# Value chunks with their own keys first, a 128-partition load for the strided values, and a regrouped start

## The chip, the cores and the metric

The kernel runs on one core of a Trainium2 chip. The metric is device time in microseconds. Three runs of the kernel before took 277.28, 278.16 and 282.28 us; their median is 278.16 us.

## The reference

Sparse attention over 8 batches of 8 heads, 576 positions and 64 dimensions a head, followed by a feed-forward block with a product of two branches:

```python
batch, n_heads, seq, head_dim = (8, 8, 576, 64)
scores = scale * np.matmul(q, k.transpose(0, 1, 3, 2))
rel = pos[:, None] - pos[None, :]
mask_local = (rel >= 0) & (rel < 32)
mask_strided = (rel >= 0) & (pos[None, :] % 32 == pos[:, None] % 32)
# heads 0 to 3 take mask_local, heads 4 to 7 mask_strided
attn = softmax(np.where(mask, scores, -1e9))
x = (attn @ v).transpose(0, 2, 1, 3).reshape(B * S, H * D)    # 4608 tokens of 512
a = x @ w1                                                    # 512 by 1024
b = x @ w2
out = (a * b @ w3) @ w_out                                    # 1024 by 1024, 1024 by 512
```

All inputs and the output are float32.

## The kernel before

Work is done for pairs of heads. A batch has four: `hp` 0 and 1 are local, 2 and 3 are strided. `pairs[4 * b + hp]` holds them, and `p0` to `p8` are the first nine.

**Local heads** are cut into 6 chunks of 96 queries (`LQ`, `LT`). Chunk c is multiplied with the 128 keys that start 32 before it, so a local tile of values, `v16L`, holds in its first 32 partitions the last keys of the chunk before, and in partitions 32 to 127 its own 96. `load_vL` loads these 96 with one DMA a head into a float32 staging tile, casts them to float16 on GpSimd in two instructions, and copies the 32 shared rows on from the chunk before (on VectorE in batch 0, on GpSimd later).

**Strided heads** are cut into 8 chunks of 72 (`SQ`, `ST`) that hold every eighth position, so that row p of `v16S` holds positions 8p to 8p+7. `load_vS` loads two heads at a time, rows 0 to 63 and rows 64 to 71 in a DMA each, and casts them in one instruction.

For a pair, `ah_T`, `ah_R` and `ph_T` transpose q and k on TensorE (with `load_rest` for the positions from 512 on), `ah_scores` and `ph_S` form scores, ScalarE takes the exponential, and `ah_PV` or `ph_PV` multiplies with the values, which carry a column of ones for the sum. `norm` divides (VectorE), and `ph_T2` transposes the result into `xT`, the feed-forward's input. In batch 0 the mask is added as a bias on TensorE before the scores (`ah_S0`: `biasL`, `biasS`); from batch 1 on the exponentials are multiplied with `maskL` or `maskS` on VectorE (`ah_S`, `ph_soft`).

**The feed-forward** goes over 9 tiles of 512 tokens. `ab_parts` gives the units of a tile: for each of 8 columns of 128, two of the a product and two of the b product; ScalarE copies a out and VectorE multiplies. `w3` and `w_out` are folded into one matrix, `w34` (`fold_tr`, `fold_mm`), and `o_parts` gives the output product.

**Order.** TensorE runs in the order of the program (`pe` keeps it). The list `stream` holds batch 0's work by hand, with small idle matmuls (`warm`) in it, and the first six units of the feed-forward's first tile; the rest of that tile, the folding and the first output tile follow, with batch 1's work put between them by `plan` (unit number, function, pair). From batch 2 on, attention is spread over the feed-forward units by `host`. The other engines' orders are set by the framework's scheduler from the dependencies. All loads go through the SP queue in the order in which the program names them: q and k of batch 0, the rest, local values, the second heads' q and k, strided values, then the weights in blocks of 512 KB, then batch 1's inputs between the last blocks of w3. Staging tiles (`stgp`) are 9.

Of the kernel before, what the change touches and what calls it, by code (L numbers as in the profile page):

```python
# [19 lines left out]
def kernel(  # L20
# [33 lines left out]
    LC = 384  # L54
    PTG = S + 64
# [16 lines left out]

    def copy(eng, out, in_):
        if eng == "a":
            nc.scalar.copy(out=out, in_=in_)  # L75
        elif eng == "v":
            nc.vector.tensor_copy(out=out, in_=in_)  # L77
        else:
            nc.gpsimd.tensor_copy(out=out, in_=in_)  # L79
# [6 lines left out]
    maskL = consts.tile([P, LQ], FP16)  # L86
    nc.gpsimd.memset(maskL, 1.0)
    nc.gpsimd.affine_select(out=maskL, in_=maskL, compare_op=ALU.is_ge,
                            fill=0.0, base=32, pattern=[[1, LQ]], channel_multiplier=-1)
    nc.gpsimd.affine_select(out=maskL, in_=maskL, compare_op=ALU.is_ge,  # L90
                            fill=0.0, base=-1, pattern=[[-1, LQ]], channel_multiplier=1)

    sel = consts.tile([4, 18, 4], FP16)
# [5 lines left out]
    causal = consts.tile([SQ, SQ], FP16)  # L99
# [8 lines left out]
    biasL = consts.tile([P, LQ], FP16)  # L108
# [12 lines left out]
    nc.vector.memset(kT[:, 0:2, 0:32], 0.0)  # L121
    nc.vector.memset(kT[:, 2:4, S:KW], 0.0)
    for i in range(2):
        nc.vector.memset(v16L[i][:, :, :, D], 1.0)
        nc.vector.memset(v16L[i][0:32, :, 0, :], 0.0)
        nc.vector.memset(v16S[i][:, :, :, D], 1.0)
    for i in range(2):
        nc.vector.memset(ptms[i][:, S:PTG], 0.0)
        nc.vector.memset(ptms[i][:, 2 * S:PTW], 0.0)
# [55 lines left out]
    def load_vL(b, hps=(0, 1)):  # L185
        vt = v16L[b % 2]
        for hp in hps:
            hs = slice(2 * hp, 2 * hp + 2)
            st = stgp.tile([P, 2, LT, D], FP32, tag="stg")
            for h in range(2):  # L190
                nc.sync.dma_start(st[32:P, h], v[b, 2 * hp + h].rearrange("(t p) d -> p t d", p=LQ))
            for pr in (bass.ds(32, 32), bass.ds(64, 64)):
                nc.gpsimd.tensor_copy(out=vt[pr, hs, :, 0:D], in_=st[pr])  # L193
            copy("p" if b else "v", vt[0:32, hs, 1:LT, 0:D], vt[96:P, hs, 0:LT - 1, 0:D])

    def load_vS(b):
        vt = v16S[b % 2]
        for hp in range(2):
# [12 lines left out]
    for b in range(B):  # L211
        for hp in range(4):
# [3 lines left out]
            s.n1 = NB // s.w  # L216
            s.kr = P if s.local else SQ
            pairs.append(s)

    def half_rows(u):  # L220
        return slice(64 * u, 64 * u + 64)

    def ph_T(s, rest, pt):
# [20 lines left out]
        def out():  # L244
            for i, (eng, t) in enumerate(engs):
                pi = ps[:, :, i * 256:i * 256 + 256]
                if s.local:
                    c0 = 32 * i
                    copy(eng, t[:, s.hp, c0:c0 + NM].rearrange("x (u p c) -> x u p c", u=2, c=4),
# [6 lines left out]
            if rest:  # L256
                for i, (eng, t) in enumerate((("a", qT), ("v", kT))):
                    pr = ps[:, i, 512:768].rearrange("x (g r) -> x g r", g=4)
                    c0 = 32 * i + NM
                    copy(eng, t[:, 0:2, c0:c0 + NR], pr[:, 0:2])  # L260
# [5 lines left out]
    def ph_S(s):  # L266
        w, kr, n, n1 = s.w, s.kr, s.n, s.n1
# [4 lines left out]
        def sc(h, c):  # L272
            r = half_rows(h)
            o = sps[:, h, c * w:(c + 1) * w] if c < n1 else pt[:, h, LC:LC + w]
            pe(nc.tensor.matmul(o, kT[r, s.hp, w * c:w * c + P], qT[r, s.hp, w * c:w * c + w],  # L275
# [10 lines left out]

    def ph_soft(s, pt):
        w, kr, n, n1 = s.w, s.kr, s.n, s.n1
# [3 lines left out]
        mk = maskL if s.local else maskS  # L292
        m1 = 2 * n1 * w
        for lo, hi, src in ((0, m1, sps[0:kr, 0:2, 0:n1 * w]), (m1, 2 * S, pt[0:kr, :, LC:LC + w])):
            nc.scalar.activation(out=pte[0:kr, lo:hi], in_=src, func=AF.Exp, bias=0.0, scale=scale)  # L295
        nc.vector.tensor_mul(ptm[0:kr, 0:2 * S].rearrange("p (a x) -> p a x", x=w),  # L296
                             pte[0:kr].rearrange("p (a x) -> p a x", x=w),
                             _ap(mk, 0, [[mk.ap[0][0], kr], [0, 2 * n], [1, w]]))

    def ph_PV(s):  # L300
        w, kr, n, n1 = s.w, s.kr, s.n, s.n1
# [3 lines left out]
        for cs in (list(range(m)), list(range(m, n))):  # L305
# [8 lines left out]
            for i, c in enumerate(cs):  # L314
                for h in range(2):
                    c0 = (h * n1 + c) * w if c < n1 else (2 * n1 + h) * w
                    pe(nc.tensor.matmul(xps[:, h, i * 65:i * 65 + 65], s.ptm[0:kr, c0:c0 + P],  # L317
                                        vt[0:kr, 2 * (s.hp % 2) + h, c, :], start=True, stop=True))
            norm(s, xps[0:w, :, 0:l * 65], cs[0], l)

    def ah_T(s):
# [5 lines left out]
        for i, nm in enumerate("qk"):  # L327
            src = x16[(s.b, nm, s.hp // 2)]
# [4 lines left out]
        for i, t in enumerate((qT, kT)):  # L333
            eng = "v" if i and s.b == 0 else "a"
            if s.local:
                c0 = 32 * i
                copy(eng, t[:, s.hp, c0:c0 + NM].rearrange("x (p c) -> x p c", c=4),
# [5 lines left out]
    def ah_R(b):  # L343
# [11 lines left out]
        for i, t in enumerate((qT, kT)):  # L355
            c0 = 32 * i + NM
            eng = "v" if i and b == 0 else "a"
            parts = [(t[:, 0:2, c0:c0 + NR], pvs[0][:, :, i]),
# [7 lines left out]

    def ah_scores(s, g, outs, kn, first):
        w, m = s.w, s.n // 2
        for i in range(m):
            ks = w * (g * m + i)  # L370
            for h in range(2):
                r = half_rows(h)
                pe(nc.tensor.matmul(outs[h][0:kn, i * w:(i + 1) * w], kT[r, s.hp, ks:ks + kn],
                                    qT[r, s.hp, ks:ks + w], start=first, stop=first or i == m - 1))

    def ah_S0(s, g, wide=True):
        w, kr, m = s.w, s.kr, s.n // 2
        bias = biasL if s.local else biasS
        if wide:
            sps = psB.tile([P, 2, NB], FP32, tag="big", name="sps")  # L380
            outs = [sps[:, 0], sps[:, 1]]
        else:
            outs = [psF.tile([P, NB], FP32, tag="f", name="sph") for _ in range(2)]
# [378 lines left out]
```

## Time and profile before

| | |
|---|---|
| median of three runs | 278.16 us |
| profiled execution, its own time | 278.08 us |
| its span, first to last instruction | 276.2 us |
| granted TensorE clock over the span | 1.000 |
| TensorE busy | 261.8 us, 95% |
| ScalarE, VectorE busy | 147.8 and 147.6 us |
| GpSimd busy | 115.6 us, 42%, ending about 160 us in |
| DMA | 48.68 MB, mean 176 GB/s |

Times in lists are microseconds from the start of the span. L416 is line 416 of the kernel before. In the timeline a line has start, duration, engine, line, operation, output and input tile, their shapes, and in brackets the idle time of the engine before it with what ended it. In busy time by stretches, the columns are the stretch, its length, the busy time of PE (matmul), PEld (weight load), DVE (VectorE), ACT (ScalarE) and POOL (GpSimd), then the granted clock, the DMA share and the DMA rate in GB/s.

### The profile page before, as it was taken

The page shows a single profiled execution, that of the slowest core. Times are in us where ns is not written, and L with a number is a line of the kernel's source. Part 1 is how long each engine was busy: PE and PEld are TensorE (multiplying, and loading weights), DVE is VectorE, ACT ScalarE, POOL GpSimd, SP SyncE. Part 2 cuts the span into 40 slices and gives each one's busy share as a digit, 9 for nine tenths or more (in the row PEclk, how much of TensorE's full clock was granted, in tenths as well). Part 3 has the DMA queues.
Part 4 walks back from the last instruction along what each step waited for, and adds up shares of the span by engine and source line. Part 5 has one row for each costly group of instructions (what it writes and reads, how often), then busy time and mean ns, then how long its engine had stood idle before and what let it go on. Part 6 is the DMA issues. An engine that isn't in the chain of part 4 may idle for free.

```text
span 276.2 us, 6648 instructions
## 1 busy us (share of the span) xinstructions
PE 261.8 (95%) x2656; PEld 138.4 (50%) x2656; DVE 147.6 (53%) x281; ACT 147.8 (54%) x298; POOL 115.6 (42%) x134
## 2 busy tenths in 40 slices
PE   1888999999899999999999999999999999999995
PEld 0465455554455555555555455555555555444442
DVE  2465452566767556755874667466547653431430
ACT  1664335857666565555556655656665654324322
POOL 4586785787958762785693734100000000000000
PEclk9999999999999999999999999999999999999999
DMA  7999999999899859897997860310031012003004
GB/s 202 268 324 391 390 385 263 268 243 234 265 282 277 219 187 267 180 297 208 256 261 219 245 137 2 116 39 2 2 115 40 0 40 114 0 2 152 0 4 152
DMA packets 56753, 48.68 MB, mean 176 GB/s; under 512 B 29201, under 2 KB 45841, under 8 KB 56721
## 3 DMA queue, kind: packets, MB, share of 16 engines
q1 hardware_dynamic: 51536, 38.87, 53.3%
q10 hardware_dynamic: 5184, 9.37, 9.3%
q8 instruction: 21, 0.34, 0.6%
q14 instruction: 12, 0.09, 0.1%
HBM read 38.80 MB, written 9.44 MB: 175 GB/s over the span
## 4 chain that ended last, share of the span: by engine, by line
PE 88%; DVE 5%; ACT 3%; DMA 2%; issue 1%; SPq 1%; DVEq 0%
PE ops L490 24%; PE aps L463 23%; PE bps L474 22%; PE sps L317 4%; PE ps L434 3%; DMA st<-in_k_dram 2%; DVE xqs L427 2%; PE sps L275 2%; DVE ptm L403 2%; PE pt L232 2%; PE xps L416 1%; PE pt L275 1%; PE tps L331 1%; PE trp L532 1%; ACT pte L402 1%
## 5 line engine op out<-in xcount | busy, mean ns | idle before, releaser
L474 PE MATMUL bps<-xT,w2h 128*128 128x512 f16 x288 | 76.2, 379 | 0.0
L463 PE MATMUL aps<-xT,w1h 128*128 128x512 f16 x288 | 74.9, 380 | 0.7 <-ACT xT L441 0.7
L477 DVE TENSOR_TENSOR abt<-bps,asb 128x512 f16<-128x512 f32 x72 | 49.5, 687 | 41.8 <-PE bps L474 28.1
L467 ACT COPY asb<-aps 128x512 f32<-128x512 f32 x72 | 43.1, 598 | 46.7 <-PE aps L463 46.7
L490 PE MATMUL ops<-w,abt 128*128 128x512 f16 x280 | 67.1, 379 | 0.0
L79 POOL CAST t<-st 128x1024 f16<-128x1024 f32 (+1 forms) x46 | 45.6, 1000 | 25.1 <-DMA st<-in_q_dram 9.8
L463 PEld LDWEIGHTS <-w1h 128*128 128x128 f16 x288 | 26.5, 98 | 29.7
L474 PEld LDWEIGHTS <-w2h 128*128 128x128 f16 x288 | 26.2, 98 | 27.7 <-issue 1.2
L490 PEld LDWEIGHTS <-abt 128*128 128x128 f16 x280 | 25.3, 98 | 26.1
L193 POOL CAST v16L<-st 32x768 f16<-32x768 f32 (+1 forms) x32 | 27.4, 858 | 14.5 <-DMA st<-in_v_dram 8.4
L501 ACT COPY osb<-ops 128x512 f32<-128x512 f32 x35 | 20.6, 588 | 18.2 <-PE ops L490 18.2
L295 ACT ACTIVATE pte<-sps 128x960 f16<-128x960 f32 (+1 forms) x24 | 23.9, 995 | 11.6 <-PE sps L275 11.6
L427 DVE TENSOR_TENSOR xqs<-sps,rcp 96x768 f16<-96x768 f32 (+1 forms) x24 | 24.4, 1017 | 0.5
L204 POOL CAST v16S<-st 72x1024 f16<-72x1024 f32 x16 | 17.1, 1070 | 16.1 <-DMA st<-in_v_dram 8.0
L296 DVE TENSOR_TENSOR ptm<-pte,maskL 128x1152 f16<-128x1152 f16 x12 | 11.7, 975 | 21.4 <-ACT pte L295 21.4
L296 DVE TENSOR_TENSOR ptm<-pte,maskS 72x1152 f16<-72x1152 f16 x12 | 11.7, 973 | 20.2 <-ACT pte L295 20.2
L441 ACT COPY xT<-ps 128x576 f16<-128x576 f16 x16 | 10.3, 641 | 22.7 <-PE ps L434 22.7
L75 ACT COPY qT<-pt 128x256 f16<-128x256 f16 (+2 forms) x48 | 17.6, 409 | 3.3 <-DVE kT L77 2.9
L317 PEld LDWEIGHTS <-ptm 72*128 72x128 f16 (+1 forms) x336 | 13.1, 97 | 6.5 <-DVE ptm L296 2.0
L490 PE MATMUL ops<-woh,w3T 128*128 128x512 f16 x64 | 15.7, 380 | 0.2 <-DVE w3T L534 0.2
L434 PEld LDWEIGHTS <-xqs 72*128 72x128 f16 (+1 forms) x224 | 12.1, 97 | 7.5 <-DVE xqs L427 0.6
L434 PE MATMUL ps<-id,xqs 72*128 72x72 f16 (+1 forms) x224 | 13.5, 200 | 0.3 <-DVE xqs L427 0.3
(93 smaller groups left out, 252.4 us busy)
## 6 DMA issues: line engine op xcount, KB each, us to landing
out_dram<-osb ACTq DMA_DIRECT2D x35, 256.0 KB, 2.0
st<-in_q_dram SPq DMA_DIRECT2D x16, 512.0 KB, 5.2
st<-in_k_dram SPq DMA_DIRECT2D x16, 512.0 KB, 5.6
st<-in_moe_w_dram SPq DMA_DIRECT2D x16, 512.0 KB, 10.4
st<-in_v_dram SPq DMA_DIRECT2D x32, 144.0 KB, 5.7
st<-in_v_dram SPq DMA_DIRECT2D x16, 256.0 KB, 8.7
st<-in_moe_w_out_dram SPq DMA_DIRECT2D x4, 512.0 KB
st<-in_q_dram SPq DMA_DIRECT2D x8, 128.0 KB, 6.3
```

Source lines behind the costliest of these rows:

```text
L79: nc.gpsimd.tensor_copy(out=out, in_=in_)
L193: nc.gpsimd.tensor_copy(out=vt[pr, hs, :, 0:D], in_=st[pr])
L295: nc.scalar.activation(out=pte[0:kr, lo:hi], in_=src, func=AF.Exp, bias=0.0, scale=scale)
L296: nc.vector.tensor_mul(ptm[0:kr, 0:2 * S].rearrange("p (a x) -> p a x", x=w), pte[0:kr].rearrange("p (a x) -> p a x", x=w), _ap(mk, 0, [[m ...
L317: pe(nc.tensor.matmul(xps[:, h, i * 65:i * 65 + 65], s.ptm[0:kr, c0:c0 + P], vt[0:kr, 2 * (s.hp % 2) + h, c, :], start=True, stop=True))
L427: nc.vector.tensor_mul(s.xqs[0:w, c0:c0 + l].rearrange("p i h d -> p h i d"), xv[:, :, :, 0:D], _ap(rcp, 0, [[rcp.ap[0][0], w], [ST, 2], [ ...
L434: pe(nc.tensor.transpose(ps[:, t * w:(t + 1) * w], s.xqs[0:w, t].rearrange("p h d -> p (h d)"), id16[0:w, 0:w]))
L463: pe(nc.tensor.matmul(st["a"], w1h[:, ci, bass.ds(jc * P, P)], xT[ci][:, tok], start=(ci == 0), stop=(ci == KM - 1)))
L467: nc.scalar.copy(out=asb, in_=st["a"])
L474: pe(nc.tensor.matmul(st["b"], w2h[:, ci, bass.ds(jc * P, P)], xT[ci][:, tok], start=(ci == 0), stop=(ci == KM - 1)))
L477: nc.vector.tensor_mul(abts[tch][:, jc, :], st["b"], st["asb"])
L490: pe(nc.tensor.matmul(st["ps"], lhs(ci), rhs(ci), start=(ci == 0), stop=(ci == KF - 1)))
```

## The change

1. A local chunk's 128 keys now start at its own first key. Its queries are 32 further on, so chunks of queries are 128, 96, 96, 96, 96 and 64 long (`QL`). `v16L` holds its own 96 keys in partitions 0 to 95 and the next chunk's first 32 after them. The cast is one instruction. The mask of local heads is stored over all 576 columns.
2. `load_vS` of batches 0 and 1 loads two heads into 128 partitions, 64 rows each, and the last 8 rows of each into another staging tile. Each cast takes every other head; the tails are copied on ScalarE (batch 0) or GpSimd (batch 1).
3. Batch 0's bias matmuls become a function of their own, `ah_bias`; those of pair 0 stand between the transposes of q and of k, and the scores of both groups of a pair are issued together.
4. The a products of three columns are issued together, by quarter, around the last transposes of a batch.
5. kT of batch 1's strided pairs is copied on VectorE; in `plan`, the transposes of batch 2's first pair come last.

The core of the diff:

```diff
+    QL = (0, 128, 224, 320, 416, 512, S)
+    QS = tuple(range(0, S + 1, SQ))
...
+    biasL = tmp[:, S:2 * S]
+    for i in range(1, LT):
+        nc.vector.tensor_copy(out=maskL[:, QL[i]:QL[i + 1]], in_=maskL[:, 32:32 + QL[i + 1] - QL[i]])
...
 def load_vL(b, hps=(0, 1)):
             for h in range(2):
-                nc.sync.dma_start(st[32:P, h], v[b, 2 * hp + h].rearrange("(t p) d -> p t d", p=LQ))
-            for pr in (bass.ds(32, 32), bass.ds(64, 64)):
-                nc.gpsimd.tensor_copy(out=vt[pr, hs, :, 0:D], in_=st[pr])
-            copy("p" if b else "v", vt[0:32, hs, 1:LT, 0:D], vt[96:P, hs, 0:LT - 1, 0:D])
+                nc.sync.dma_start(st[0:LQ, h], v[b, 2 * hp + h].rearrange("(t p) d -> p t d", p=LQ))
+            nc.gpsimd.tensor_copy(out=vt[0:LQ, hs, :, 0:D], in_=st[0:LQ])
+            copy("v" if b == 0 and hp else "p", vt[LQ:P, hs, 0:LT - 1, 0:D], vt[0:32, hs, 1:LT, 0:D])
 
     def load_vS(b):
         vt = v16S[b % 2]
+        if b < AHEAD:
+            st = stgp.tile([P, 2, ST, D], FP32, tag="stg")
+            sr = stgp.tile([P, 2, ST, D], FP32, tag="stg")
+            sv = v[b, 4:8].rearrange("(g h) (p c) d -> h p g (c d)", h=2, c=ST)
+            for g in range(2):
+                nc.sync.dma_start(st[:, g].rearrange("p c d -> p (c d)"), sv[:, 0:64, g])
+                nc.sync.dma_start(sr[64 + 32 * g:72 + 32 * g].rearrange("p h c d -> p h (c d)"),
+                                  sv[:, 64:SQ, g].rearrange("h p x -> p h x"))
+            for h in range(2):
+                nc.gpsimd.tensor_copy(out=vt[0:64, h:4:2, :, 0:D], in_=st[half_rows(h)])
+            for g in range(2):
+                copy("p" if b else "a", vt[64:SQ, 2 * g:2 * g + 2, :, 0:D], sr[64 + 32 * g:72 + 32 * g])
+            return
         for hp in range(2):
             st = stgp.tile([SQ, 2, ST, D], FP32, tag="stg")
...
     def ah_T(s, between=None):
         for i, nm in enumerate("qk"):
+            if i and between:
+                between()
...
-            eng = "v" if i and s.b == 0 else "a"
+            eng = "v" if i and (s.b == 0 or not s.local) else "a"
...
     def ab_parts(tch):
-            def a(qt, jc=jc, st=st):
+            def a(qt, jc=jc, st=st, cis=None):
+                cis = cis or (2 * qt, 2 * qt + 1)
...
+            if tch < 2 and jc < 3:
+                fine[tch].append(a)
...
-    add(ah_T, p0)
+    add(ah_T, p0, bias01)
     add(ah_R, 0)
     add(ah_T, p1)
-    add(ah_S0, p0, 0)
-    add(ah_S0, p0, 1)
-    add(ah_S0, p1, 0, False)
+    add(ah_S0, p0, (0, 1))
+    add(ah_bias, p1, 0, False)
+    add(ah_S0, p1, (0,))
     add(ah_PV, p0, 0)
-    add(ah_S0, p1, 1)
+    add(ah_bias, p1, 1)
+    add(ah_S0, p1, (1,))
     add(ah_PV, p0, 1)
     add(ah_PV, p1, 0)
     add(ah_PV, p1, 1)
+    add(ah_T, p2)
     add(ph_T2, p0)
-    add(ah_T, p2)
-    add(ph_T2, p1)
     add(ah_T, p3)
-    add(ah_S0, p2, 0)
-    add(ah_S0, p2, 1)
-    add(ah_S0, p3, 0, False)
+    add(ah_bias, p2, 0)
+    add(ah_bias, p2, 1)
+    add(ah_S0, p2, (0, 1))
+    add(ph_T2, p1)
+    add(ah_bias, p3, 0, False)
+    add(ah_S0, p3, (0,))
...
     add(ph_T2, p2)
     add(first[4])
-    add(first[2])
+    add(first[8])
     add(ph_T2, p3)
-    for i in (1, 3, 5):
+    for ci in (2, 3):
+        for f in fine[0]:
+            add(lambda f=f, ci=ci: f(1, cis=(ci,)))
+    for i in (2, 3, 6, 7, 10, 11):
         add(first[i])
...
-            (28, ah_PV, p6, 0), (29, ah_PV, p6, 1), (29, ph_TS, None, p8), (30, ah_PV, p7, 0),
-            (31, ph_T2, p6), (31, ah_PV, p7, 1))
+            (28, ah_PV, p6, 0), (29, ah_PV, p6, 1), (30, ah_PV, p7, 0), (31, ph_T2, p6), (31, ah_PV, p7, 1),
+            (31, ph_TS, None, p8))
...
-    for i in (2, 1, 3, 5):
-        tile1[i]()
+    for f in fine[1]:
+        f(1, cis=(2,))
     stream[pos[0]]()
+    for f in fine[1]:
+        f(1, cis=(3,))
```

## The prediction

> **What bounds the kernel now.** I read the page first, then the chain of work that ended last, the timeline of PE and POOL up to 80 us, busy time by stretches, and the record of when each load landed.
>
> ```profile
> span 276.2 us, 6648 instructions
> PE 261.8 (95%) x2656; PEld 138.4 (50%) x2656; DVE 147.6 (53%) x281; ACT 147.8 (54%) x298; POOL 115.6 (42%) x134
> ```
>
> PE is busy 95% of the span. By stretches it is at 5.00 of 5.00 us from 80 to 100 us, and the chain from there to the end is feed-forward matmuls. What this change can move lies before 76 us: batch 0 up to 26.7 us, and batch 1 between 45 and 76 us.
>
> The chain, in order of time, in batch 0:
>
> ```profile
> 10.30 0.48 PE sps L385 x2
> 10.78 0.36 PE sps L373 x6
> 11.14 0.59 PE sps L385 x2
> ...
> 19.82 0.26 PE xps L416 x8
> ...
> 24.82 0.65 ACT xT L441
> 25.46 0.04 issue
> 25.51 0.38 PE aps L463
> ```
>
> Bias matmuls (L385) stand on the path, then the strided pairs' value matmuls (L416), and at the end PE waits for ACT's xT. The timeline shows when the strided values are cast and first used, batch 0 and batch 1:
>
> ```profile
> 15.89 2.20 POOL L204 CAST v16S<-st 72x1024 f16<-72x1024 f32 x2 [0.21 <-DMA st<-in_v_dram]
> 18.16 1.04 POOL L79 CAST w1h<-st 128x1024 f16<-128x1024 f32 x1
> ...
> 59.54 1.04 POOL L204 CAST v16S<-st 72x1024 f16<-72x1024 f32 x1
> 60.95 1.04 POOL L204 CAST v16S<-st 72x1024 f16<-72x1024 f32 x1 [0.37 <-DMA st<-in_v_dram]
> ```
> ```profile
> 19.66 0.41 PE L416 MATMUL xps<-v16S,ptm 72*128 72x65 f16 x8
> ...
> 66.48 0.40 PE L416 MATMUL xps<-v16S,ptm 72*128 72x65 f16 x8 [0.39 <-DVE ptm L403]
> ```
>
> Batch 0's values are ready at 18.09 and used at 19.66: 1.6 us of slack. Batch 1's are ready at 61.99 and used at 66.48: 4.5 us. Both sets of casts wait for DMA. Busy time by stretches, with the DMA rate last:
>
> ```profile
> 13.50:16.50 3.00, 2.37 (x40) 1.60 (x39) 2.82 (x9) 1.19 (x3) 2.69 (x3) 1.00 1.07 233
> 17.00:20.00 3.00, 3.00 (x57) 2.20 (x57) 1.19 (x2) 2.98 (x7) 2.56 (x3) 1.00 1.07 389
> ```
>
> From 13.5 to 16.5 us the strided values come in at 233 GB/s, into 64 partitions; the weights, into 128, at 389 GB/s. DMA engines never rest until 50 us (share 0.99 in the page's slices), so whatever lengthens one load delays all behind it: SP issues a load only when the one eight before it has landed (the 25th is issued at 22.05, the 17th landed at 21.99).
>
> **Part by part.**
>
> *Masks.* The local mask grows from 96 to 576 columns: five more DVE copies and a wider bias. Nearest row 0.34 us (128x96): six times that is 2.0 us, before 8.36, where DVE idles 4.9 us. Nothing; 0.5 us if that cover went.
>
> *Local values.* Each pair of heads loses two POOL casts (0.88 and 0.83) for one (0.86): 0.86 us less POOL, twice a batch. One shift copy of batch 0 goes from DVE (0.39) to POOL (0.76). POOL reaches q and k of the strided heads (13.56 before) about 0.9 us sooner, but that k lands at 14.59, so at most 0.5 us. In batches 2 to 7 PE is full over it: 0.
>
> *Chunk widths.* 128, 96 four times, 64: still 576 columns a head in scores, transposes, exps and norms. Exps: 960 and 192 columns cost 978 and 334 ns, 0.84 ns a column, so 1024 and 128 give the same sum. 0.
>
> *Joined scores.* Four bias matmuls of pair 0 move into PE's wait for k (until 8.11): 0.48 + 0.59 = 1.07 us off the path.
>
> *a products three abreast.* Three products with ci=2 run while ACT copies xT: of 0.65 + 0.04 us waiting, 0.65 go. At 75.16 another 0.15.
>
> *Strided kT of batch 1 on DVE, the transposes of batch 2 last.* ACT's kT copy of 0.49 leaves the chain at 63.2; DVE has 4 us idle there. 0.5 us.
>
> *Strided values of batches 0 and 1.* Each of the two loads (256 KB, plus 32 KB of tail) now fills 128 partitions, but its source is walked as 2 heads by 64 rows. What decides is how many of the 16 engines such a load gets. The trace shows it by completions: loads whose outermost count is 128, 96 or 64 on both sides post 16, and the 8-row tails post 8 (plus one at issue: at 10.22, the other eight from 14.5 to 15.2). So an 8-row load is split by its rows over 8 engines. Here the source has two outermost steps and the destination 128; a split by whole steps on both sides gives two. Fast bound: 16 engines at the weights' 389 GB/s, 0.67 us a load. Slow bound: 2 engines. One engine moves 389/16 = 24.3 GB/s, so 131 KB on each take 5.4 us a load, and two loads on the same pair 10.8 us, where before this pair spent some 2.5 us on them (0.59 MB at 233 GB/s). I take the slow end: a small outermost count is what the 8-row tails have.
>
> [...]
>
> **The sum.** Half of the completions of the strided heads' k stand by 13.4 (the last at 14.59, from slow engines). Two loads after one another: 13.4 + 10.8 + 0.2 (tails) = 24.4, against 17.0. Two POOL casts of 64x1024 (1.07 each, from 72x1024) need both: 26.5. ACT's two tail copies (1.04 each, by ACT's 128x1024 cast) come on top: the second lands at 24.4, and what is queued behind it on ACT (xT of the local pairs, qT and exps of pair 2) waits too. Pair 2's value matmuls start at 26.5 instead of 19.66, +6.9; were ACT's copies ahead of qT of pair 2 (16.77, 2.9 us before 19.66), 25.5 + 2.9 = 28.4, +8.7. I take +7.5. Weights lie behind the loads on the two engines, 1.35 us each: the third at 28.4 against 21.99, +6.4, so less late than PE; no further term. Less 0.65 (a abreast). After such a gap PE also starts slower: eight transposes took 0.85 us at 9.45 and 0.46 at 17.34, though the granted clock is 1.00 in both; +0.7, an estimate (1.4 us of PE work in the first microseconds, at half pace). The bias's 1.07 is hidden in the wait. Batch 0: +7.5.
>
> Batch 1: its second value load landed at 60.59. It is late by the 6.4 that the queue already is, and by 8.3 (10.8 − 2.5) anew, less 1 of idle DMA share between 50 and 60: 74.3. Two casts and two tail copies on POOL (2.1 each pair): 78.5. PE, 7.5 late, wants it at 74.0: +4.5, the 0.5 of kT hidden in it. Lower bound 1 (the queue recovers, tails early), upper 7. DMA moves only 252 to 274 GB/s between 40 and 60, so it recovers some: I take 3.4, a third of the way to the lower bound. Next late are q and k of batch 2: three more casts after 78.5, so by 81.7, wanted at 71.5 + 11 = 82.5, covered, because their transposes now come last.
>
> Span 276.2 + 7.5 + 3.4 = 287.1. The profiled execution took 278.08 us, 1.9 more than its span, and the median of the runs is 278.16, so no correction between the two: **289.0 us**.
>
> **Rivals.**
>
> *A. The loads run on all sixteen engines* (not slower). Then values land 1 us sooner, and 1.07 + 0.65 + 0.15 + 0.5 = 2.4 us come off, less about 1 us for ACT's tail copies (2.1 us, in a stretch where ACT is busy 3.75 of 5): 276.7 us; 274 to 279. For it: the destination is 128 partitions, as the weights'. Against: eight completions for eight rows. It decides if the first new load lands before 16 us.
>
> *B. Two engines, but batch 1 pays nothing:* DMA there moves only 252 to 274 GB/s, some of it waiting for buffers, and the slack of 4.5 us with PE's own delay covers it. 278.1 + 7.5 − 0.5 = 285 us; 282 to 287. Against: POOL waited for DMA at 60.95.
>
> *C. Two engines, and ACT or POOL blocked longer* by the tail copies in their queues, so batch 0 costs 8.7 + 1 and batch 2's loads add 2: 278.1 + 9.7 + 3.4 + 2 = 293 us.
>
> **How the numbers follow.** Forecast 0.46 (own range 284 to 293), A 0.24, B 0.22, C 0.08. A measurement of this kernel tells about 2% (5.6 us: 272.6 and 283.7) from no change. Slower: 0.46 + 0.08 + 0.8 × 0.22 = 0.72. Same: 0.2 × 0.22 + 0.83 × 0.24 = 0.24. Faster: the rest of A, 0.04. The cases have both signs, so the range takes most of A at the low end and half of C at the high end: 276 to 294.
>
> **What would show it.** The new value loads take over 8 us from issue to landing, or 16-engine loads behind them show a few engines some 6 us late; POOL's strided casts of batch 0 start near 24 us, idle before them released by DMA of v; the page's slices show DMA rate falling well under 200 GB/s around 19 to 24 us; L416's first 72-row matmuls start near 26.5 and near 78; from about 90 us on the two traces run parallel. It is wrong if batch 0's casts start before 17 us (A), or if the first weights' casts are not late. The bias matmuls stand before 8.1 us in every case, and POOL's busy time falls by about 14 us less the tails.

## The result and the profile after

The changed kernel takes 294.85 us (median of four runs, 293.68 to 295.58) against 277.9 us for the kernel before beside it: a ratio of 1.061, 95% interval 1.056 to 1.067. It is slower by 17 us, where 289.0 were forecast and 294.0 was the upper end of the range. Here and below, times are medians of all runs of a kernel; ratios leave out runs more than 1.5% above the fastest of the same kernel, and are against runs of the kernel before made beside them. Lines of this part are those of the changed kernel: L80, L82 and L84 are copies and casts on ScalarE, VectorE and GpSimd, L213 casts the strided values, L119 makes the biases, L415 is the bias matmuls, L453 multiplies with the values in batch 0 and 1, L472 is the last transposes, L503 and L514 the a and b products, L507 the copy of a. In some of the experiments they lie one or two lines further on.

The page of the changed kernel, the share of each engine and the granted clock in 40 slices:

```profile
span 292.4 us, 6639 instructions
PE 266.9 (91%) x2656; PEld 142.0 (49%) x2656; DVE 146.9 (50%) x286; ACT 148.3 (51%) x298; POOL 104.8 (36%) x121
...
PEclk9995599999999999999999999999999999999999
```

The span grew by 16.2 us and TensorE's busy time by only 5.1. So 11 us are new idle time, and the busy time grew although the same 2656 matmuls run: two slices have half the clock, where the kernel before had none. Of the chain of work that ended last (start, length, what; steps under 0.4 us are left out), 88% was TensorE before and 2% DMA; now 68% and 20%. It goes through the new loads:

```profile
10.34 16.75 DMA st<-in_v_dram
27.21 1.05 POOL v16S L213
28.31 1.05 POOL v16S L213
29.84 9.15 DMA st<-in_moe_w_dram
...
62.90 14.75 DMA st<-in_v_dram
...
78.87 1.16 POOL v16S L213
```

The timeline of GpSimd around batch 0's values, to be read against the casts at 15.89 of the kernel before:

```profile
14.11 1.04 POOL L84 CAST t<-st 128x1024 f16<-128x1024 f32 x1 [0.54 <-DMA st<-in_k_dram]
27.21 2.14 POOL L213 CAST v16S<-st 64x1024 f16<-64x1024 f32 x2 [12.06 <-DMA st<-in_v_dram]
29.41 1.04 POOL L84 CAST w1h<-st 128x1024 f16<-128x1024 f32 x1
```

GpSimd stood still for 12 us. The landing records say why. Each of the new 256 KB loads posts two completions (and one at issue). In batch 0 the first lands at 18.97 and 19.63, the second at 26.26 and 27.09; in batch 1 at 68.90 and 71.73, and at 75.06 and 77.65. The first block of weights behind them has fourteen of its sixteen completions by 19.67 and the other two only at 27.75 and 28.38. Busy time by stretches, the last three columns being granted clock, DMA share and GB/s:

```profile
14.00:16.00 2.00, 0.74 (x22) 0.53 (x17) 1.53 (x5) 0.67 (x2) 1.04 (x1) 1.00 0.16 58
...
30.00:37.00 7.00, 6.94 (x69) 4.59 (x68) 3.49 (x8) 1.28 (x2) 6.13 (x7) 0.51 0.94 319
```

From 14 to 16 us the DMA share is 0.16, which is 2.6 of 16 engines, at 58 GB/s: by its two completions two engines carry a load, and the rest have hardly anything to do. And from 30 to 37 us TensorE is busy all the time, at half its clock.

All matmuls of the two traces can be paired, since both have the same number in each group. How late the paired ones are tells where the time went. "Stretch" is from the eighth strided value matmul to the first folding product:

| late against the kernel before, us | changed kernel |
|---|---|
| eighth value matmul of pair 2 (19.87 before) | +9.8 |
| first folding product (38.25) | +12.4 |
| last local value matmul of batch 1 (59.18) | +12.5 |
| last value matmul of pair 7 (71.26) | +12.6 |
| first b product of the second tile (74.19) | +15.7 |
| first output product of the second tile (90.69) | +14.2 |
| last output product (272.90) | +16.1 |

So 9.8 us are the values, 2.6 come in the stretch after them, 1.7 between there and the second tile's outputs, and 1.9 bit by bit in the last 180 us. The last of these is in no step of the forecast.

### The profile page after: what moved, and what is told of

The parts are those of the page before. It is cut to its first block, busy times and chain, and to the rows that moved or that the text cites. A ratio compares the mean times of both kernels' runs of the same rounds, so it can differ in the third digit from the quotient of the medians.

```text
span 292.4 us, 6639 instructions
## 1 busy us (share of the span) xinstructions
PE 266.9 (91%) x2656; PEld 142.0 (49%) x2656; DVE 146.9 (50%) x286; ACT 148.3 (51%) x298; POOL 104.8 (36%) x121
## 4 chain that ended last, share of the span: by engine, by line
PE 68%; DMA 20%; SPq 3%; POOL 2%; DVE 2%; ACT 2%; issue 1%; POOLq 0%
PE aps L503 19%; PE bps L514 19%; PE ops L532 19%; DMA st<-in_v_dram 14%; DMA st<-in_moe_w_dram 7%; PE sps L339 3%; PE ps L472 3%; PE sps L290 2%; PE pt L248 2%; SPq L198 1%; POOL v16S L213 1%; PE pt L290 1%; DVE xqs L464 1%; SPq L178 1%; POOL t L84 1%
## 5 line engine op out<-in xcount | busy, mean ns | idle before, releaser
L514 PE MATMUL bps<-xT,w2h 128*128 128x512 f16 x288 | 75.5, 379 | 1.5 <-ACT asb L507 1.5
L503 PE MATMUL aps<-xT,w1h 128*128 128x512 f16 x288 | 75.6, 385 | 0.1
L507 ACT COPY asb<-aps 128x512 f32<-128x512 f32 x72 | 42.9, 599 | 46.9 <-PE aps L503 42.4
L84 POOL CAST t<-st 128x1024 f16<-128x1024 f32 (+1 forms) x46 | 46.2, 1011 | 31.6 <-DMA st<-in_k_dram 13.6
L503 PEld LDWEIGHTS <-w1h 128*128 128x128 f16 x288 | 26.5, 98 | 29.9 <-issue 0.9
L514 PEld LDWEIGHTS <-w2h 128*128 128x128 f16 x288 | 26.0, 97 | 29.7 <-issue 2.3
L319 ACT ACTIVATE pte<-sps 128x1024 f16<-128x1024 f32 (+1 forms) x24 | 24.5, 1021 | 13.5 <-PE sps L290 13.5
L464 DVE TENSOR_TENSOR xqs<-sps,rcp 128x768 f16<-128x768 f32 (+1 forms) x24 | 24.5, 1021 | 0.5
L309 DVE TENSOR_TENSOR ptm<-pte,maskS 72x1152 f16<-72x1152 f16 (+1 forms) x16 | 13.6, 848 | 22.2 <-ACT pte L319 20.4
L309 DVE TENSOR_TENSOR ptm<-pte,maskL 128x1152 f16<-128x1152 f16 (+2 forms) x16 | 13.3, 834 | 21.2 <-ACT pte L319 20.6
L80 ACT COPY qT<-pt 128x256 f16<-128x256 f16 (+2 forms) x48 | 17.6, 409 | 3.1 <-DVE kT L82 2.8
L199 POOL CAST v16L<-st 96x768 f16<-96x768 f32 x16 | 13.7, 856 | 14.8 <-DMA st<-in_v_dram 8.6
L223 POOL CAST v16S<-st 72x1024 f16<-72x1024 f32 x12 | 12.8, 1065 | 15.5 <-PE pm L339 13.1
L472 PEld LDWEIGHTS <-xqs 72*128 72x128 f16 (+2 forms) x224 | 13.2, 99 | 9.2 <-DVE xqs L464 1.8
L472 PE MATMUL ps<-id,xqs 72*128 72x72 f16 (+2 forms) x224 | 15.5, 203 | 0.2
L532 PE MATMUL ops<-woh,w3T 128*128 128x512 f16 x64 | 15.7, 380 | 0.0
```

Of the source, the lines that this page charges most:

```text
L309: nc.vector.tensor_mul(o.rearrange("p (a x) -> p a x", x=w), i.rearrange("p (a x) -> p a x", x=w), mk)
L319: nc.scalar.activation(out=pv[0:kr, :, lo:hi], in_=src, func=AF.Exp, bias=0.0, scale=scale)
L464: nc.vector.tensor_mul(s.xqs[0:w, c0:c0 + l].rearrange("p i h d -> p h i d"), xv[:, :, :, 0:D], _ap(rcp, 0, [[rcp.ap[0][0], w], [ST, 2], [ ...
L472: pe(nc.tensor.transpose(ps[:, s.q[t]:s.q[t + 1]], s.xqs[0:l, t].rearrange("p h d -> p (h d)"), id16[0:l, 0:l]))
L503: pe(nc.tensor.matmul(st["a"], w1h[:, ci, bass.ds(jc * P, P)], xT[ci][:, tok], start=(ci == 0), stop=(ci == KM - 1)))
L507: nc.scalar.copy(out=asb, in_=st["a"])
```

## The experiments

**Which part of the change costs.** Four kernels isolate the load. In `e2` the kernel before gets the new `load_vS` and nothing else. In `e3` and `e4` the changed kernel has it in one batch only, in `e5` in none.

```diff
-        if b < AHEAD:      # changed kernel, load_vS
+        if b < 1:          # e3: new load in batch 0 alone
+        if b == 1:         # e4: in batch 1 alone
+        if b < 0:          # e5: in none
```

> The kernel before with only the load of strided values of batches 0 and 1 taken from the change. Few engines: two completions a load, batch 0's values about 10 us late, granted clock 0.5 for 10 us or more, 288 to 294 us. Rival, the regrouped order causes it: 277 to 281 us.

> The changed kernel with the new load in batch 0 alone; batch 1 loads its strided values as before. If batch 1's late values are covered because PE is already 12.5 us late: 291 to 295 us, that is within 3 us of the changed kernel. If batch 1 pays on its own: 285 to 290 us.

> The changed kernel with the new load in batch 1 alone. With PE on time nothing covers it: the values land near 71 us, are cast by 75, and are wanted near 66; 286 to 292 us. Rival, slack in batch 1 takes it in any case: 278 to 283 us.

> The changed kernel with the strided values of batches 0 and 1 loaded as before (72 partitions, two heads a load, casts on GpSimd); everything else of the change stays. Theory: the loads make about 13 of the 16.8 us, and the rest of the change is a loss of its own: the late bias (PV of pair 0 at 13.21 against 12.96, k's transposes 1.5 us late) and the three a products that fill the psF buffers after batch 1 (+2.5 to 3.7). 278.1 + 0.3 to 1 + 2.5 to 3.7 - 0.65 = 281 to 283. Rival 1, the prediction's own sum for the rest (bias hidden, a products in ACT's time, kT on DVE): 278.1 - 1.3 = 277. Rival 2, only the loads cost: 278.

| | median, us | ratio to before, interval |
|---|---|---|
| e2, new load alone | 293.4 | 1.056 (1.052 to 1.059) |
| e3, batch 0 alone | 291.4 | 1.050 (1.047 to 1.053) |
| e4, batch 1 alone | 288.5 | 1.034 (1.023 to 1.046) |
| e5, rest of the change alone | 281.9 | 1.016 (1.012 to 1.020) |

The new load alone makes nearly the whole loss, and the rest of the change is a small loss too, where the forecast had a gain. The two batches do not add up: over `e5`, batch 0 alone costs 0.034 of the time, batch 1 alone 0.019, both together 0.045. In `e4` the output products of the second tile are 7.6 us late, and before batch 1's strided work it was 1.8; so late values cost 5.8 us there (part of it at a granted clock of 0.5 from 69.62 to 76.45). In the changed kernel the same load costs 1.7 by the trace (+12.4 at the first folding product, +14.2 at these outputs; `e3` has +11.1 at both), and TensorE itself comes 12.5 us later there: most of batch 1's lateness hides behind batch 0's. By the ratios it is more: `e3`, without it, is 0.012 lower, some 3.2 us. But 1.4 us of that already lie between the two profiled runs at the first folding product, before batch 1's values are used.

**Whether it is the number of engines.** `e1` splits each new load by heads. The same bytes go to the same 128 partitions, but 64 rows are outermost on both sides:

```diff
-                nc.sync.dma_start(st[:, g].rearrange("p c d -> p (c d)"), sv[:, 0:64, g])
+                for h in range(2):
+                    nc.sync.dma_start(st[half_rows(h), g].rearrange("p c d -> p (c d)"), sv[h, 0:64, g])
```

> The changed kernel with each of its 128-partition value loads issued as two, one a head, so that source and destination both have 64 rows outermost; same bytes, same partitions, same casts. Few engines: every such load posts 16 completions, both pairs have landed by 17 us instead of 27.1, the first strided value matmuls start before 20.5 us instead of 28.3, the granted clock stays at 1.00, and the time falls by 11 us or more, to 278 to 283 (the 3.7 us lost between 84 and 92 us may stay). Rival, the regrouped order or the tail copies on ACT cause the loss: the time stays above 289.

It took 285.7 us, ratio 1.027 (1.021 to 1.034). The casts of batch 0 start at 16.24 instead of 27.21, as the theory wants, and 9 us are gone; but 7.6 more than the kernel before is too much for it, and the value matmuls start at 23.07 and not before 20.5. What was left became the next questions.

`e11` goes the other way round: it keeps one DMA a load, but walks the source as four heads by 32 rows.

```diff
+            s4 = v[b, 4:8].rearrange("h (p c) d -> h p (c d)", c=ST)
-                nc.sync.dma_start(st[:, g].rearrange("p c d -> p (c d)"), sv[:, 0:64, g])
+                nc.sync.dma_start(st[:, g].rearrange("p c d -> p (c d)"), s4[:, 32 * g:32 * g + 32])
...
+                for h in range(4):
+                    copy("p", vt[32 * g:32 * g + 32, h, :, 0:D], st[32 * h:32 * h + 32, g])
```

> The changed kernel with each new load of 256 KB walked as four heads by 32 rows instead of two heads by 64 (the same bytes; GpSimd's casts become eight of 32x512 instead of two of 64x1024). Theory (the outermost count of the source sets how many engines carry the load): four completions instead of two, each engine carries 65 KB: the first load lands near 16.5 instead of 19.6 and the second 3 to 3.7 us later, at 19.5 to 20.2 instead of 27.1; value matmuls of pair 2 near 22 to 24 instead of 28.3; 288 to 290 us. Rival: the load is slow for another reason (a partition-crossing destination, the tails between), lands near 27 as before, and the time stays near 295.

Each load now posts four completions, and the time is 289.85 us, ratio 1.044 (1.038 to 1.049). GpSimd's timeline:

```profile
19.68 2.56 POOL L84 CAST v16S<-st 32x512 f16<-32x512 f32 x4 [3.78 <-DMA st<-in_v_dram]
24.53 2.60 POOL L84 CAST v16S<-st 32x512 f16<-32x512 f32 x4 [2.29 <-DMA st<-in_v_dram]
```

The number of completions went with the outermost count of the source: two gave two, four gave four, 64 gave sixteen. The time fell as expected, the landings less so: the first load lands at 19.62, no sooner than with two engines, and the second 4.86 us later at 24.48, instead of 7.46 later. Half the bytes on each engine did not halve the time (4.86 against 7.46 us). The rate was 18 GB/s an engine for the second load in the changed kernel (131 KB in 7.46 us) and 13.5 here; 14 to 20 us move 200 to 223 GB/s here over a DMA share of 1.05, so weights moved at the same time.

**The loss between batch 1 and the second tile.** The three a products take all three PSUM buffers `psF`, and b waits for ACT's copy of a. The changed kernel's timeline:

```profile
89.94 1.89 PE L514 MATMUL bps<-xT,w2h 128*128 128x512 f16 x8 [1.25 <-ACT asb L507]
```

A theory was that this junction costs 2.5 to 3.7 us (the step from +12.6 to +15.7 above). `e6` and `e8` put the order of the kernel before back there, on top of the old loads and of the split loads:

```diff
-            (28, ah_PV, p6, 0), (29, ah_PV, p6, 1), (30, ah_PV, p7, 0), (31, ph_T2, p6), (31, ah_PV, p7, 1),
-            (31, ph_TS, None, p8))
+            (28, ah_PV, p6, 0), (29, ah_PV, p6, 1), (29, ph_TS, None, p8), (30, ah_PV, p7, 0), (31, ph_T2, p6),
+            (31, ah_PV, p7, 1))
...
-    for i in (0, 4, 8):
+    stream[pos[0]]()
+    tile1[0]()
+    tile1[4]()
+    ph_T2(p7)
+    for i in (2, 1, 3, 5):
         tile1[i]()
-    ph_T2(p7)
-    for f in fine[1]:
-        f(1, cis=(2,))
-    stream[pos[0]]()
-    for f in fine[1]:
-        f(1, cis=(3,))
...
```

> As the run before it, and the first products of the second tile and the transposes of pair 8 in the order of the kernel before (no three a products abreast after batch 1; those of batch 0 stay). Theory of the buffers: the loss between batch 1 and 2 goes, 2.5 to 3 us less than the run before: 278 to 280. Rival: that loss only follows from late data, there is none with the old loads, and this run equals the one before within 0.6 us.

> The changed kernel with each new load split by heads, so that 64 rows are outermost on both sides, and the order after batch 1 of the kernel before. Theory of the buffers: 2.5 us less than with the split loads alone (285.7): 283. Rival: the same 285.7 within 0.8 us. In both the rest above 278 is the half clock where it appears, ACT's tail copies of 1.04 us each ahead of xT, and the late bias.

The theory fell. `e6` took 281.6 us against 281.9, `e8` 285.1 against 285.7: the same. The wait of 1.25 us is real, but the a products that caused it were done ahead of their turn. With the old loads, TensorE is 0.5 us early at the last value matmul, 2.3 late at the first b product and 0.8 late at the first output product; in the order of before it is 1.2, 1.2 and 1.5 late (`e6` had lost 1.3 us at half clock in batch 0, which `e5` had not). A stretch of late events that comes back a tile later is a changed order and no loss.

**The loss of 0.4 us a batch.** From one tile to the next, the changed kernel and `e5` fall behind by 0.4 us, while `e2`, which has the old local chunks, falls behind by 0.2 in all of them together (from the second tile's outputs to the end). In each batch two local pairs have their last six transposes. TensorE's timeline of one such group, kernel before, changed kernel, and `e9`:

```profile
105.25 0.42 PE L434 MATMUL ps<-id,xqs 96*128 96x96 f16 x6
105.50 0.60 PE L474 MATMUL bps<-xT,w2h 128*128 128x512 f16 x2
```
```profile
119.43 0.52 PE L472 MATMUL ps<-id,xqs 128*128 128x128 f16 x6
119.89 0.61 PE L514 MATMUL bps<-xT,w2h 128*128 128x512 f16 x2
```
```profile
105.74 0.43 PE L472 MATMUL ps<-id,xqs 128*128 128x128 f16 x6
106.01 0.60 PE L514 MATMUL bps<-xT,w2h 128*128 128x512 f16 x2
```

From the first transpose to the next product it is 0.257 us before and 0.455 us after. The trace has the place: the sixth transpose has 64 rows; its weight load starts only 134 ns after the matmul before it (2 ns for the others), and the next product comes 132 ns after it (43 before). `e9` makes the sixth one 96 rows wide (the extra columns are not read), with the old strided loads:

```diff
-            l = s.q[t + 1] - s.q[t]
-            pe(nc.tensor.transpose(ps[:, s.q[t]:s.q[t + 1]],
+            l = max(s.q[t + 1] - s.q[t], w)
+            pe(nc.tensor.transpose(ps[:, s.q[t]:s.q[t] + l],
```

> The changed kernel with the old strided loads (281.9 us), and the last of the six transposes of a local pair taken over 96 rows instead of 64. In the traces the six transposes of a local pair take 257 ns from their start to the next matmul before the change and 455 ns after it: the one with 64 rows starts 138 ns after the one before it instead of 42, and the matmul behind it 132 ns later. Theory: this is the loss of 0.4 us a batch that the traces show from batch 2 to 7; 12 pairs by 0.198 = 2.4 us less: 279.5. Rival: what grows there belongs to another part (score chunks of 128, 96 and 64), and the time stays at 281.9 within 0.6.

279.34 us, ratio 1.007 (1.003 to 1.010): 2.6 us less, where 12 groups by 0.198 us are 2.4. A group that went from 96 rows to 64 and back to 128 paid 0.09 us at each of the two changes (138 ns from start to start instead of 42, then 132 instead of 43), and going from 128 to 96 cost next to nothing (0.270 us a group in `e9`, 0.257 in the kernel before). The same price stands elsewhere in the traces: after 100 us in the kernel before, the matmul behind a product of 128x512 starts 216 ns after it when it has 72, 96 or 128 rows, and 309 ns after it when it has 64 (medians of 645 and 19). Why 64 rows cost this is not shown: the trace has the starts alone.

**The stretch after the values: clock or late weights.** Of the sixteen completions of each of the first three weight loads, two come 7 to 9 us behind the rest, as if they stood behind the values on the same two engines. So the late weights and the clock could both have made the 2.6 us. The kernels `e7`, `e13`, `e14` and `e15` give TensorE idle matmuls while it waits:

```diff
+    def keep_busy(n):
+        ps = psF.tile([P, P], FP32, tag="f", name="busy")
+        for _ in range(n):
+            pe(nc.tensor.matmul(ps, id16, id16, start=True, stop=True))
...
+    add(keep_busy, 135)    # 85 in e13 and e14, 140 in e15
     add(warm, 3)
     add(ah_PV, p2, 0)
```

> The changed kernel with 135 idle matmuls of 128x128 on TensorE (about 8 us, into a PSUM tile of their own) ahead of the value matmuls of pair 2, in the time in which TensorE waits for them. Theory: the granted clock of 0.5 from 23.14 to 36.80 us follows from the empty stretch from 19.6 us on and costs about 2.7 us; with TensorE kept busy the clock stays at 1.00 there and 292 us come out (291 to 293). Rival 1: the half clock has another cause, the granted clock is 0.5 again, and the time is 294.9. Rival 2: the clock stays, but the weights, late on two engines (third at 31.0 us), set the start of the feed-forward, and the time falls by under 1 us.

> The changed kernel with 85 idle matmuls instead of 135 ahead of the value matmuls of pair 2, so that they end before the values are cast (22.4 + 5.5 = 27.9 us, at 65 ns each as the 135 took). Theory: with the clock at 1.00 the stretch from the second half of those value matmuls (29.4) to the first folding product takes 18.7 us as in the kernel before, instead of 21.3: folding starts at 48.1 instead of 50.7. Then batch 1's values, which land at 77.65 at the latest and are cast until 79.9, hold TensorE, so that only part of the 2.6 reaches the end: 293 to 294.5 us. Rival 1: all of it reaches the end, 292.2. Rival 2: folding still starts near 50.7, the weights set it: 294.9.

> As the run before it, and the old strided load in batch 1 (with the new load in batch 0 alone and no idle matmuls the time was 291.4 us, granted clock 0.5 from 20.78 to 34.44). Theory: batch 1 no longer holds TensorE, so the 2.5 us of the clock come off the end: 288.9 (288.4 to 289.6). Rival: the half clock was not what stretched the time from the values to the folding, the weights late on two engines were: 291 or more.

> The new load in batch 0 alone, with 140 idle matmuls ahead of the value matmuls of pair 2. In the run with 85 they started at 19.93 and were over at 24.8, a gap of 2.7 us stayed, and the granted clock fell to 0.5 at 27.99. At 58 ns each 140 reach from 19.9 to 28.0, up to the values at 27.7. Theory: no gap, the clock stays at 1.00 past 28 us, the stretch from the values to the first folding product falls from 20.6 us to 18.7, and the time from 291.4 to about 289.5 (288.7 to 290.2). Rival 1: the stretch stays at 20.6 or more with the clock at 1.00, so the late weights set it: 291.4. Rival 2: the clock falls all the same (a slow stretch earlier makes the idle matmuls overshoot, as the 135 did): 291 to 292.5, and the size of the term rests on the stretches alone.

`e7` took 295.3 us, `e13` 294.3, `e14` 291.7 and `e15` 290.2. By their times alone the first three show nothing, and none went by its plan. In `e7` the matmuls ahead of the idle ones already ran at half pace (four bias matmuls in 1.17 us, 0.66 in the changed kernel), so the idle ones ended at 31.2, two us after the last cast of the values (28.9). (This trace's first clock record starts at 24.70; a view shows 1.00 where there is no record.) In `e13` and `e14` they were over 3.6 and 2.7 us too soon, and after that gap the clock was at 0.5 from 29.64 and from 27.99. Only in `e15` did they reach up to the values, at 27.4, and its time is at the upper end of what was expected. The traces decide. The stretch, and how much of it lies in a granted clock of 0.5:

| kernel | stretch, us | of it at clock 0.5 |
|---|---|---|
| before | 18.38 | 0 |
| e5, old loads | 18.50 | 0 |
| e6, old loads | 19.80 | 3.41 |
| e7, 135 idle matmuls | 18.51 | 0 |
| e15, 140 | 18.51 | 0 |
| e3 | 20.08 | 5.16 |
| e14, 85 | 20.32 | 5.70 |
| e2 | 20.47 | 6.24 |
| e13, 85 | 21.09 | 6.83 |
| changed kernel | 21.00 | 7.09 |

With the full clock the stretch is what it was before the change, 0.13 us apart, although the first weight loads are late in two completions all the same: the third block is complete at 30.1 in `e15`, 30.6 in `e3` and 31.0 in the changed kernel, 1.5, 1.3 and 1.3 us after the eighth value matmul (2.1 us after it in the kernel before, so against TensorE the weights are not late). Each us at half clock adds 0.30 to 0.39 to the 18.5. `e5` and `e6` show it without any late load: both have the old ones and the same order up to here, and in `e6` the clock was at 0.5 from 21.98 to 25.40. So it is the clock. By stretches, changed kernel and `e15`, then `e6` and `e5` (granted clock third from the right):

```profile
29.40:50.71 21.31, 20.93 (x142) 11.21 (x142) 8.68 (x16) 6.78 (x12) 17.34 (x17) 0.83 1.02 349
```
```profile
28.40:47.09 18.69, 17.90 (x142) 9.20 (x141) 8.55 (x16) 6.78 (x12) 15.46 (x15) 1.00 1.01 367
```
```profile
20.34:40.14 19.80, 19.02 (x141) 10.20 (x138) 8.68 (x16) 6.96 (x13) 14.59 (x14) 0.91 1.04 391
```
```profile
20.44:38.94 18.50, 17.72 (x141) 9.01 (x138) 8.56 (x16) 6.96 (x13) 13.55 (x13) 1.00 1.04 393
```

The same 142 matmuls are busy for 20.93 and for 17.90 us, the same 141 for 19.02 and 17.72. What this is worth at the end rests on the traces: `e15` stands at a ratio of 1.048 (1.043 to 1.053) and `e3` without idle matmuls at 1.050 (1.047 to 1.053), so the gain of about 2 us in the profiled spans (287.8 against 289.7) is not told apart by the times.

**The rest of `e1`.** Its clock was 0.5 from 15.96 to 29.61 in the profiled run, and the first of ACT's two tail copies (1.04 us, at 20.51) stood in the queue ahead of an exponential of pair 2 and xT of pair 1, so that the value matmuls came at 23.07, long after their casts. On top of `e1`, `e10` puts the tails on VectorE and widens the last transpose:

```diff
-                copy("p" if b else "a", vt[64:SQ, ...
+                copy("p" if b else "v", vt[64:SQ, ...
```

> The changed kernel with each new load split by heads (64 rows outermost on both sides, 285.7 us), the tail copies of batch 0 on VectorE instead of ScalarE, and the last transpose over 96 rows. Theory: 2.4 us go with the transposes; ScalarE's two tail copies (1.04 each) no longer stand ahead of the exponentials and xT of pair 1, so the value matmuls of pair 2 start near 20.5 instead of 23.08: another 1 to 2.5 us; 281 to 282.3. Rival: the rest of the loss is the half clock from about 16 us on, which a run has or has not, and the tail copies were not in the way: 283.3 or more, value matmuls still near 23.

```profile
16.08 2.13 POOL L214 CAST v16S<-st 64x1024 f16<-64x1024 f32 x2 [1.13 <-DMA st<-in_v_dram]
...
18.14 0.69 DVE L82 CAST v16S<-sr 8x1024 f16<-8x1024 f32 x1
...
20.14 0.41 PE L454 MATMUL xps<-v16S,ptm 72*128 72x65 f16 x8
```

279.44 us, ratio 1.006 (1.003 to 1.009), less than expected, and the granted clock was 1.00 from 13 us to the end. The value matmuls start at 20.14. Of the 6.3 us between `e1` and `e10`, 2.4 to 2.6 are the transposes; how much of the rest is the tails and how much the clock, these two runs do not tell. But `e10` equals `e9` (279.34), the same order with the old loads and the wide transposes: with rows outermost and the tails off ScalarE, loading into 128 partitions is neither a loss nor a gain, and the whole change comes to within 0.6% of the kernel before.

**The start.** `e12` has the old loads, the wide transpose, the local bias in a tile of its own (worked out on GpSimd) and pair 1's transposes in their old place:

```diff
-    biasL = tmp[:, S:2 * S]
+    biasL = tmb[:, S:2 * S]      # a second tile
...
+        (nc.gpsimd if bias is biasL else nc.vector).tensor_scalar(...)
```

> The changed kernel with the old strided loads, the last transpose over 96 rows, the local bias in a tile of its own and worked out on GpSimd (so that the bias matmuls no longer hold up k's transposes), and pair 1's last transposes ahead of pair 3's q and k as in the kernel before. Theory: 281.9 - 2.4 (transposes) - 0.6 (value matmuls of pair 2 at 19.7 instead of 20.23) - 0 to 1 (bias inside the wait for k, the prediction's step) = 278 to 279. Rival: the bias off the path gains its full 1.07 and the three a products 0.65: 276.5 to 277.5. Second rival: nothing of the start counts, since the first weights set it: 279.5.

279.2 us, ratio 1.007 (1.003 to 1.010), nearest to the second rival. The value matmuls of pair 2 come at 19.19, 0.46 us sooner than in the kernel before and 1.1 sooner than in `e9`, and the first folding product 0.3 sooner than before. But the total is that of `e9`: what is gained before batch 1 has gone by the second tile's outputs (+0.3 in `e12`, +0.5 in `e9`). No version here beats the kernel before.

## Why the prediction was right or wrong

*Right: the mechanism.* The load was taken as two engines; it has two completions, the first lands at 19.0 and 19.6 (18.8 by the forecast's terms), GpSimd waits for v, weights behind it are late, and the traces do drift apart at batch 0. `e1` and `e11` show that it is the outermost count (64 rows gave 16 completions, four heads 4). Two of the signs named did not come: from 18 to 24 us the DMA rate was 259 to 305 GB/s, not under 200 (the low stretch was 14 to 16 us), and from 90 us on the traces were not parallel. GpSimd's busy time fell by 10.8 us; forecast were about 14 less the tails.

*The first step that failed: 10.8 us for two loads.* That both loads share one pair of engines was the author's estimate; no run shows which engines carry a load, only that the second's two completions came 7.29 and 7.46 us after the first's. The first was in time. The second was put at the same 5.4 and landed 7.46 us after the first, so both were there at 27.1 and not at 24.4. The rate of 24.3 GB/s an engine was read from a stretch in which all engines carry the same load. While weights moved beside it, the second load had 18 on each of its two (131 KB in 7.46 us); why, stays open. The casts started at 27.21 and the value matmuls were 9.8 us late, 2.3 more than the +7.5 taken for them.

*The second: "+0.7" for a slow start after the gap.* The kind of loss was right and the size was not. It was 2.5 us of the stretch's 2.6: not a microsecond at half pace but 13.65 us of half clock, of which 7.1 fell into the stretch. The row under it was misread, too: the trace of the kernel before has its first clock record at 14.03, so the 1.00 shown at 9.45 is a stretch without a record, and nothing there tells the clock apart from another slow start. These two steps make batch 0 +12.4 instead of +7.5.

*Batch 1, +3.4.* It was 1.7 by the trace. The bounds of 1 to 7 held. The values landed later than forecast (77.65, not 74.3), but TensorE was 12.4 us late and not 7.5, and so waited only twice:

```profile
78.86 0.19 PE L453 MATMUL xps<-v16S,ptm 72*128 72x65 f16 x1 [0.28 <-POOL v16S L213]
80.06 0.37 PE L453 MATMUL xps<-v16S,ptm 72*128 72x65 f16 x7 [1.01 <-POOL v16S L213]
```

That the term was too large is luck for the sum: it took 1.7 us off the error. Rival B, which had nothing for batch 1, was as far off as the forecast. The new load in batch 1 alone costs 5.8 there (`e4`).

*The third: "Chunk widths ... 0".* The columns are the same, as worked out, but the sixth transpose has another row count: 2.4 us over batches 2 to 7 by the length of the groups, 2.6 by `e9`; 1.9 of them lie behind the second tile's first output. The step counted columns, and the price here hung on the rows (216 ns against 309, above).

*Bias and a products.* TensorE no longer waits for xT at the a products (0.5 us before, nothing after; 0.2 on a's copy instead). The bias was not ready in the wait for k. VectorE had it in its queue behind a cast that waited for k:

```profile
8.18 0.43 DVE L82 CAST t<-st 128x512 f16<-128x512 f32 x1 [4.86 <-DMA st<-in_k_dram]
8.52 0.30 DVE L119 TENSOR_SCALAR tmp<-maskL 128x576 f16<-128x576 f16 x1
...
8.87 0.69 PE L415 MATMUL sps<-tmp,id 128*128 128x320 f16 x2 [1.61 <-DVE tmp L119]
```

So k's transposes start at 9.79 instead of 8.11. "Nothing; 0.5 us if that cover went" was wrong about the masks in kind: VectorE idles 4.9 us there, but the idle time is a wait at the head of its queue, and the bias stands behind it. Its price is small all the same, since the local value matmuls come only 0.25 us later (13.21 against 12.96).

*The sum.* 9.83 + 2.62 + 1.74 + 1.93 = 16.12 us against 10.9: values and clock too small by 4.9, batch 1 too large by 1.7, transposes missing by 1.9. The other 0.7 to the median is that the profiled run (294.13) was faster than it. Rival C came nearest to the time (293) by a cause that does not hold: its tail copies block ACT (4.61 us of waiting ahead of the second), but the values are late for the load's sake.

## What to carry to other kernels

Before a load is reshaped, compare the outermost counts of both sides: a source of two steps put 256 KB on two engines, for 5.6 us (19.63, counted from the landing of k at 14.06) and 7.5 us, and the next three loads had two of their sixteen completions 7 to 9 us later than the others. Price a wait of TensorE with what follows it: beyond the gap itself, half clock added about a third of a us for each us. Look for single matmuls of 64 rows between others of 96 or 128 (0.09 us at each side here), and compare traces by paired matmuls, since only a lag that stays is a loss.

## What the runs showed of the hardware that was not expected

- SP's queue was held up by the two-engine loads: the issue of the second tail took 4.22 us (from 10.94), and no weight was issued before 15.28, so that the DMA share fell to 0.16. In the six other kernels with this load in batch 0 the issue took 4.05 to 4.44 us; with four engines it took 0.49, with sixteen 0.48. The two lines are the changed kernel and `e11`:

```profile
10.94 4.22 SPq L210 DMA_DIRECT2D sr<-in_v_dram  x1
```
```profile
10.49 0.49 SPq L211 DMA_DIRECT2D sr<-in_v_dram  x1
```

- The granted clock was at 0.5 for 3.41, 6.83, 10.24 or 13.65 us at a time, which is about one, two, three and four times 3.41. In batch 0 of `e4` and `e6` the clock returned after 3.41 us (at 25.40 in `e6`); but in the changed kernel TensorE was busy 6.94 of 7.00 us from 30 to 37 us and the clock returned only at 36.79, and in `e1` it was busy 12.83 of 14.00 us from 16 to 30 us at a mean clock of 0.51. So 6.8 us of a nearly always busy TensorE did not bring the clock back there sooner, and what brings it back stays open.
- That the clock fell in `e1` at 15.96 without any long gap is not explained, nor that it fell in `e8` at 15.85 and in `e4` and `e6` near 21.9, where batch 0's values were in time. The four runs of `e1` had mean clocks of 0.976, 0.982, 0.988 and 0.994 and took 286.30, 286.64, 285.13 and 282.96 us. In `e5` two runs with 1.000 took 281.29 and 280.89 us, and two with 0.994 took 282.53 and 282.74.
- A cast of 8 partitions by 1024 took 1.04 us on ScalarE and on GpSimd, as long as one of 128 partitions (1.04 on both), and 0.69 us on VectorE (`e10`).
- Why the second load had 18 GB/s on each engine, and the four-engine load 13.5, stays open beyond the fact that weights moved beside them.
